# Attention followed by two MLPs on one core: where the 1e-9 of the softmax sum is added, and where the first unit of weights is converted

## The chip, the core and the metric

The kernel runs on one core of a Trainium2 chip. The metric is device time in microseconds (us) of the one launch, and smaller is better. The engines that matter are TensorE (PE, with its weight loads PEld), VectorE (DVE), ScalarE (ACT), GpSimd (POOL) and the sync engine (SP), which issues every DMA of this kernel.

## The reference

Three stages run one after the other, all in float32:

```
q_assign = argmax(q_n . c_n); k_assign = argmax(k_n . c_n)      # 16 clusters per head
scores = 0.125 * q k^T,  -1e9 where the clusters differ         # 2 batches, 8 heads, 768 x 768, head size 64
attn = exp(scores - rowmax);  attn = attn / (sum(attn) + 1e-9)
x = attn @ v                                                    # [1536, 512]
x = max(x@w1, x@w2, x@w3) @ w_out                               # 512 -> 768 -> 512
x = leaky_relu(x@w_in, 0.01) @ w_out                            # 512 -> 2048 -> 512
```

The change touches the `+ 1e-9` of the third line and the preparation of the weights of the fifth.

## The kernel before

**Precision.** Every matmul runs in the float32r format. An operand is split into a high part and a rest (`eh`/`el`, `xh`/`xl`, `wh`/`wl`), and products of the parts are summed in PSUM.

**Attention.** Work comes in 48 units n = 0..47. A unit is 256 queries (two blocks of 128) of one head of one pair of heads; six units make a pair, and there are eight pairs. The letters in `ORDER` name the operations of a unit:

- `S` (L415): four score matmuls of one block of 128 queries; `M` (L422): the row maximum on VectorE; `X` (L428): the exponential on ScalarE, which also writes the row sum.
- `RA` (L438, function `guard`): VectorE adds 1e-9 to the two sums; `RC` (L443): the reciprocal; `RB` (L450): widening on GpSimd.
- `T` (L463): transposes on TensorE; `E`, `B`, `L` (L480, L484, L492, L495): splitting the transposed exponentials into `eh` and `el` on ScalarE, VectorE and GpSimd.
- `V` (L506): twelve matmuls with the values into `o`; `Y`, `K1`, `K2` (L525, L531, L535): out of PSUM into `acc`.
- `G` (L293): similarities to the centroids, two groups of twelve matmuls per pair of heads, for the pair after next.
- `D0`, `D1` (L376): DMAs on SP that stack the operands `q1, q2, k1, k2` of the next pair.

**What sets the order.** The program is written out by hand. `ORDER` has one row of operations for each of the six units of a pair (row r = n mod 6), `op/lag` works on unit n - lag, and `ONCE` adds operations at (unit, position in the row). Every engine runs its own instructions in this order. So an operation that VectorE gets in the middle of a row stands in front of all that VectorE does later in that row.

**Weights.** The MLP weights come in 14 units, each [128, 2048]. A unit is fetched and converted in four pieces c = 0..3 of 512 columns. `Weights.fetch` (L127) issues two DMAs from SP, `raw` and `low`, into one of two slots, taken in turn; a slot is free again once its piece is converted. `Weights.piece` (L144) is a generator of seven VectorE operations (L151, L152, L153, L156, L157, L158, L165; five are TENSOR_SCALAR) and two of ScalarE (L155, L164); each `yield` is a place where it can stop. During attention `take_apart` (L554) advances a piece by one `next` for each `wcX` in `ONCE`. So the pieces of unit 0 are converted in groups of three, three and one operation of VectorE. In the MLP `step` (L167) advances pieces between matmuls.

**MLPs.** From L756 on TensorE runs 36 or 24 matmuls for each chunk of 512 tokens and each weight unit (L782 to L784), with weights of later units converted in between. `split_x` (L771) makes `xh` and `xl` out of `acc` first; its VectorE operations are L774.

Of the kernel before, what the change touches and what calls it, by code (L numbers as in the profile page):

```python
# [8 lines left out]
F32 = mybir.dt.float32  # L9
# [3 lines left out]
ALU = mybir.AluOpType  # L13
AX = mybir.AxisListType
# [3 lines left out]
P = 128  # L18
# [33 lines left out]
ONCE = {  # L52
# [15 lines left out]
}  # L68
WAYS = ("DPP", "DDP", "DPA", "DDP", "DDP", "DPA")
ENGINE = {"QH": "A", "QH@1": "P", "KH": "P", "VH": "P", "KL": "P", "KL@0": "D", "VL": "P", "W": "P", "W@1": "D"}  # L70
WARM = (8, 4, 4, 4)
# [10 lines left out]
def clustered_attention_mlps(  # L82
# [16 lines left out]
    nc = tc.nc  # L99
    PSUM = bass.MemoryType.PSUM  # L100

    const = ctx.enter_context(tc.tile_pool(name="const", bufs=1))
    accp = ctx.enter_context(tc.tile_pool(name="acc", bufs=1))
    wa = ctx.enter_context(tc.tile_pool(name="wa", bufs=1))
# [7 lines left out]
    class Weights:  # L112
# [31 lines left out]
        def piece(self, raw, u, pool, c):  # L144

            high, low = raw[0][:, :, 1], raw[1][:, :, 0]
            x = self.rawp.tile([P, WP], F32, tag="wx", name=f"wx{u}_{c}", bufs=2)
            t = self.rawp.tile([P, WP], F32, tag="wt", name=f"wt{u}_{c}", bufs=3)
            xi, ti, lowf = x.bitcast(U32), t.bitcast(U32), low.bitcast(F32)
            ts, stt = nc.vector.tensor_scalar, nc.vector.scalar_tensor_tensor  # L150
            ts(low, low, 0x01FFFFFF, None, op0=ALU.bitwise_and)  # L151
            ts(xi, high, 0x7FFFFFFF, None, op0=ALU.bitwise_and)  # L152
            ts(x, x, W_LEAST, W_MOST, op0=ALU.max, op1=ALU.min)  # L153
            yield 1.5
            nc.scalar.activation(lowf, low, AF.Copy, scale=2.0**-36)  # L155
            ts(ti, xi, 3, 0x3FFFF000, op0=ALU.logical_shift_left, op1=ALU.bitwise_and)  # L156
            stt(xi, high, 0xC0000000, ti, op0=ALU.bitwise_and, op1=ALU.bitwise_or)  # L157
            ts(ti, xi, 0xFF800000, None, op0=ALU.bitwise_and)  # L158
            yield 2
            if c == 0:  # L160
                wh[u] = pool.tile([P, UW], F32R, tag=f"wh{u % 4}", name=f"wh{u}")
                wl[u] = pool.tile([P, UW], F32R, tag=f"wl{u % 4}", name=f"wl{u}")
            hi, lo = wh[u][:, c * WP : (c + 1) * WP], wl[u][:, c * WP : (c + 1) * WP]
            nc.scalar.copy(hi, x)  # L164
            nc.vector.tensor_tensor(lo, lowf, t, op=ALU.mult)  # L165

        def step(self):  # L167


            passes = 0  # L170
            for _ in range(3):
                self.turn = (self.turn - 1) % 3
                if self.turn == 0:
                    if len(self.going) < 2 and self.todo and self.todo[0][::2] in self.raw:
                        u, pool, c = self.todo.pop(0)
                        g = self.piece(self.raw.pop((u, c)), u, pool, c)
                        self.going.append([0, g])
                at = [g for g in self.going if g[0] == self.turn]
                if at:
                    at[0][0] += 1  # L180
                    passes = next(at[0][1], 0)
                    if not passes:
                        self.going.remove(at[0])
                        passes = 1
                    break
            self.load()
            return passes
# [11 lines left out]
    weights = Weights(wraw, [wraw, wraw])  # L199


    with ExitStack() as att:
# [6 lines left out]
        sm = att.enter_context(tc.tile_pool(name="sm", bufs=2))  # L209
# [7 lines left out]
        gain = const.tile([2 * 2 * C, 1], F32, name="gain")  # L217
        base = const.tile([2 * 2 * C, 1], F32, name="base")
        cb = const.tile([P, NP, 2 * C], F32, name="cb")

        st = {}

# [60 lines left out]
        def bank():  # L283

            st["bank"] = st.get("bank", -1) + 1
            ps = ps_s.tile([P, 1024], F32, tag="s", name=f"s{st['bank']}")
            return ps[:, 0:S], ps[:, S:1024]
# [111 lines left out]
        un = {}  # L399

        def unit(n):
            p, r = divmod(n, 2 * NG)
            j, g = divmod(r, NG)
            return p, j, g

        def scores(n, i):
            p, j, g = unit(n)
            q1, q2, k1, k2 = st[p][j]
            if i == 0:
                un[n] = {"e": [], "sum": sm.tile([P, 2], F32, tag="ssum", name=f"ssum{n}", bufs=4)}  # L410
            c0 = g * G + i * P
            ps, spare = bank()
            for a, b, start in ((q1, k1, True), (q2, k2, False)):
                for lo, hi in ((0, 512), (512, S)):
                    nc.tensor.matmul(  # L415
                        ps[:, lo:hi], a[:, c0 : c0 + P], b[:, lo:hi], start=start, stop=not start
                    )
            un[n]["s", i], un[n]["spare", i] = ps, spare
# [6 lines left out]
        def exps(n, i):  # L425
            u = un[n]
            e = ep.tile([P, S], F32, tag="ee", name=f"ee{n}_{i}")
            nc.scalar.activation(  # L428
                e, u.pop(("s", i)), AF.Exp, bias=u.pop(("m", i)), scale=1.0,
                accum_out=u["sum"][:, i : i + 1],  # L430
            )
            u["e"].append(e)

        def guard(n):
            p, j, g = unit(n)
            if "rs" not in st[p]:
                st[p]["rs"] = sm.tile([P, NG, 2, 2], F32, tag="rs", name=f"rs{p}")
            nc.vector.tensor_scalar_add(st[p]["rs"][:, g, :, j], un[n]["sum"], 1e-9)  # L438

        def inverse(n):  # L440
            p, j, g = unit(n)
# [29 lines left out]
        def way(n, k):  # L471
            return WAYS[n % (2 * NG)][k // 2]

# [79 lines left out]

        def take_apart(op):  # L554

            if op in ("wF", "wL"):
                for c in (0, 1) if op == "wF" else (2, 3):
                    weights.fetch(0, c)
                return
            if op == "wN":  # L560
                for c in (0, 1):
                    weights.fetch(1, c)
                return
            c = int(op[1])
            if c not in pieces:
                pieces[c] = weights.piece(weights.raw[0, c], 0, wa, c)
            next(pieces[c], None)

        def do(op, at):

# [36 lines left out]
            elif o == "D":  # L607
                operands(at, 3 * d)
            elif o == "S":
                scores(at, d)  # L610
            elif o == "M":
                maxima(at, d)
            elif o == "X":
                exps(at, d)
            elif op == "RA":
                guard(at)
# [28 lines left out]
        pieces, scraps = {}, {}  # L645
        with tc.manual_schedule():
# [44 lines left out]

            oh0 = sm.tile([P, D + NQ * 4 * C], BF16, tag="oh", name="oh0", bufs=1)
            nc.vector.memset(oh0[:, 0:D], 0.0)
            st[0]["oh"] = oh0

            def start(op):
# [36 lines left out]
            for n in range(-4 * NG, NU + 6):  # L733
                c, r = divmod(n, 2 * NG)
                items = ORDER[r].split()
                for i in range(len(items) + 1):
# [7 lines left out]
                    if "/" in items[i]:  # L744
                        op, lag = items[i].split("/")
                        at = n - int(lag)
                        if 0 <= at < NU:
                            do(op, at)
                    else:
                        op, ahead = items[i].split("+")  # L750
                        at = c + int(ahead)
# [151 lines left out]
```

## Time and profile before

| | us |
|---|---|
| median of 3 runs | 734.15 (731.75 to 734.33) |
| the profiled execution, its own time | 735.01 |
| its span, first to last instruction | 733.2 |

| engine | busy us | share of the span | instructions |
|---|---|---|---|
| PE | 709.1 | 97% | 3873 |
| PEld | 607.0 | 83% | 3873 |
| DVE | 557.5 | 76% | 1003 |
| ACT | 374.5 | 51% | 717 |
| POOL | 283.8 | 39% | 264 |

The share is an average over two stages: attention up to about 265 us, the MLPs after it. The mean granted clock of TensorE is 0.987 of full speed. In the rows further down, "x4" is a number of instructions, a name on the left of `<-` is written and one on the right is read, and a bracket at a row's end is idle time of that engine just before the instruction with what ended it. Starts are us from the span's start.

### The profile page before, as it was taken

Reading aid. Unit: us, or ns where it says so; the run is one execution under the profiler, and the core shown is the slowest. Engines: PE = TensorE matmul, PEld = TensorE weight load, DVE = VectorE, ACT = ScalarE, POOL = GpSimd, SP = SyncE. Lnnn points to the kernel's source line nnn. Section 1 sums busy time; section 2 is a strip of 40 time slices with the busy share of each in tenths; the row PEclk is TensorE's granted clock in tenths of the full one; section 3 lists DMA queues with packets and bytes.
Section 4 is the critical chain, followed back from the end, with each engine's and each line's share of the span. In section 5 each row is a group of like instructions: output and inputs, shape, how many; then the busy total and the mean of one; then the engine's idle time right before and its main releaser. Section 6 shows DMA issues by size and latency. Waiting matters only on the chain.

```text
span 733.2 us, 10794 instructions
## 1 busy us (share of the span) xinstructions
PE 709.1 (97%) x3873; PEld 607.0 (83%) x3873; DVE 557.5 (76%) x1003; ACT 374.5 (51%) x717; POOL 283.8 (39%) x264
## 2 busy tenths in 40 slices
PE   7999989998999689999999999999999999999997
PEld 5899979987999678888888888888888888888886
DVE  6798999998999988779877289878619954983222
ACT  2788969877899774433323034446434432432220
POOL 1778768776887551011101110323212322222220
PEclk9799999999999999999999999999999999999999
DMA  8976444452444114645556045416414540610112
GB/s 221 284 188 164 99 129 116 111 141 66 107 110 137 58 58 134 232 131 178 161 169 193 8 135 156 149 51 216 162 53 136 179 145 29 199 59 1 44 42 88
DMA packets 30150, 92.37 MB, mean 126 GB/s; under 512 B 4528, under 2 KB 4528, under 8 KB 30096
## 3 DMA queue, kind: packets, MB, share of 16 engines
q1 hardware_dynamic: 30096, 91.67, 42.0%
q8 instruction: 31, 0.51, 0.3%
q14 instruction: 23, 0.19, 0.1%
HBM read 68.16 MB, written 3.15 MB: 97 GB/s over the span
## 4 chain that ended last, share of the span: by engine, by line
PE 86%; DVE 9%; ACT 2%; issue 2%; DMA 0%; POOL 0%; ACTq 0%; POOLq 0%
PE h L784 12%; PE h L783 12%; PE h L782 12%; PE y L783 8%; PE y L782 8%; PE y L784 8%; PE s L415 8%; PE o L506 7%; PE t L463 6%; DVE mx L422 2%; PE s L293 1%; DVE el L492 1%; ACT ee L428 1%; DVE xl L774 1%; DVE rs L438 1%
## 5 line engine op out<-in xcount | busy, mean ns | idle before, releaser
L812 POOL TENSOR_TENSOR hl<-a,hh 128x512 fp32r<-128x512 f32 x66 | 91.0, 1378 | 346.0 <-ACT hh L811 346.0
L784 PE MATMUL h<-xh,wl 128*128 128x512 f32 x408 | 158.9, 389 | 0.0
L782 PE MATMUL h<-xh,wh 128*128 128x512 f32 x408 | 158.8, 389 | 0.0
L783 PE MATMUL h<-xl,wh 128*128 128x512 f32 x408 | 158.7, 389 | 0.0
L811 ACT CAST hh<-a 128x512 fp32r<-128x512 f32 x66 | 41.1, 622 | 127.2 <-DVE a L805 76.4
L782 PE MATMUL y<-hh,wh 128*128 128x512 f32 x264 | 102.7, 389 | 0.0
L783 PE MATMUL y<-hl,wh 128*128 128x512 f32 x264 | 102.7, 389 | 0.0
L784 PE MATMUL y<-hh,wl 128*128 128x512 f32 x264 | 102.7, 389 | 0.0
L428 ACT ACTIVATE ee<-s,mx 128x768 f32<-128x768 f32 x96 | 86.8, 905 | 28.0 <-DVE mx L422 26.8
L495 POOL TENSOR_TENSOR el<-et,eh 128x512 fp32r<-128x512 f32 x72 | 98.2, 1369 | 5.3 <-ACT et L480 2.5
L422 DVE TENSOR_REDUCE mx<-s 128x1 f32<-128x768 f32 x96 | 91.1, 950 | 11.6 <-PE s L415 5.1
L415 PE MATMUL s<-k,q 128*128 128x512 f32 (+3 forms) x384 | 92.9, 366 | 3.5 <-ACT tmp L525 1.8
L783 PEld LDWEIGHTS h<-xl,wh 128*128 128x128 f32 x408 | 76.6, 188 | 15.9
L782 PEld LDWEIGHTS h<-xh,wh 128*128 128x128 f32 x408 | 76.6, 188 | 15.9
L784 PEld LDWEIGHTS h<-xh,wl 128*128 128x128 f32 x408 | 76.6, 188 | 15.8
L803 ACT COPY a<-h 128x512 f32<-128x512 f32 x66 | 38.6, 585 | 94.3 <-PE h L784 92.5
L506 PE MATMUL o<-eh,vs 128*128 128x256 f32 x288 | 75.4, 294 | 11.7 <-DVE acc L535 6.9
L463 PE MATMUL t<-idf,ee 128*128 128x128 f32 x576 | 81.0, 279 | 2.5 <-DVE el L492 2.3
L836 DVE TENSOR_TENSOR acc<-y,acc 128x512 f32<-128x512 f32 x72 | 48.5, 686 | 41.1 <-PE y L784 41.1
L807 DVE SCALAR_TENSOR_TENSOR a<-a,h 128x512 f32<-128x512 f32 x48 | 32.8, 684 | 61.7 <-ACT a L803 61.6
L506 PE MATMUL o<-el,vs 128*128 128x256 f32 x288 | 73.2, 286 | 0.0
L463 PEld LDWEIGHTS t<-idf,ee 128*128 128x128 f32 x576 | 66.7, 145 | 5.8 <-DVE el L492 3.3
(97 smaller groups left out, 1179.2 us busy)
## 6 DMA issues: line engine op xcount, KB each, us to landing
raw<-in_w SPq DMA_DIRECT2D x56, 512.0 KB, 4.2
low<-in_w SPq DMA_DIRECT2D x56, 511.5 KB, 3.5
q<-qh SPq DMA_DIRECT2D x32, 192.0 KB, 3.3
k<-kh SPq DMA_DIRECT2D x32, 192.0 KB, 3.7
rq<-in_qT SPq DMA_DIRECT2D x8, 384.0 KB, 3.7
rk<-in_kT SPq DMA_DIRECT2D x8, 384.0 KB, 3.8
q<-ql SPq DMA_DIRECT2D x16, 192.0 KB, 4.0
k<-kl SPq DMA_DIRECT2D x16, 192.0 KB, 3.5
```

The source lines that it names most:

```text
L415: nc.tensor.matmul(ps[:, lo:hi], a[:, c0 : c0 + P], b[:, lo:hi], start=start, stop=not start)
L422: nc.vector.tensor_reduce(mx, un[n]["s", i], axis=AX.X, op=ALU.max, negate=True)
L428: nc.scalar.activation(e, u.pop(("s", i)), AF.Exp, bias=u.pop(("m", i)), scale=1.0, accum_out=u["sum"][:, i : i + 1],)
L463: nc.tensor.transpose(ps[:, kk, i * P : (i + 1) * P], u["e"][i][:, (k + kk) * P : (k + kk + 1) * P], idf,)
L495: nc.gpsimd.tensor_tensor(lo, et, hi.bitcast(F32), op=ALU.subtract)
L506: nc.tensor.matmul(u["o"], vs[:, t, :], u[e][:, t, :], start=(t == 0 and e == "eh"), stop=(t == NQ - 1 and e == "el"),)
L782: nc.tensor.matmul(ps, ah, bh, start=(k == 0), stop=False)
L783: nc.tensor.matmul(ps, ah, bl, start=False, stop=False)
L784: nc.tensor.matmul(ps, al, bh, start=False, stop=(k == n - 1))
L811: nc.scalar.copy(hh[:, f, :], a)
L812: nc.gpsimd.tensor_tensor(hlo[:, f, :], a, hh[:, f, :].bitcast(F32), op=ALU.subtract)
L836: nc.vector.tensor_tensor(a, ps, a, op=ALU.add)
```

## The change

1. The row sums get four fixed tiles `sums` of [128, 2, 2], filled with 1e-9 once at the start by four memsets on VectorE. The exponential writes its sum into the first of each two numbers, and the 1e-9 stays beside it. `guard` becomes a TENSOR_REDUCE that adds the two, where it was a TENSOR_SCALAR that added a constant.
2. `piece` gets four more `yield`s, so that every VectorE operation of it is a step of its own. `step` runs over the new ones, so the MLP's pace stays.
3. In `ONCE` unit 0's pieces are now `w00`, `w01`, `w02`, `w03`: one step at position 20 of each unit n = 3..9, 10..16, 17..23, 24..30 (before: between n = 14 and n = 51). The fetches stand one by one: `f00`, `f01` at n = 1, `f02` at n = 9, `f03` at 16, and the first two pieces of unit 1 (`f10`, `f11`) at 23 and 30 (before: two at n = 1, two at n = 40, and unit 1's at n = 51).

```diff
-    (0, 7): "KH@1", (0, 8): "QL@1", (1, 11): "wF", (14, 12): "w0a", (15, 20): "w0b",
...
+    (1, 11): "f00", (1, 12): "f01", (3, 20): "w00", (4, 20): "w00", (5, 20): "w00", (6, 20): "w00",
...
             ts(low, low, 0x01FFFFFF, None, op0=ALU.bitwise_and)
+            yield 0
             ts(xi, high, 0x7FFFFFFF, None, op0=ALU.bitwise_and)
+            yield 0
             ts(x, x, W_LEAST, W_MOST, op0=ALU.max, op1=ALU.min)
             yield 1.5
             nc.scalar.activation(lowf, low, AF.Copy, scale=2.0**-36)
             ts(ti, xi, 3, 0x3FFFF000, op0=ALU.logical_shift_left, op1=ALU.bitwise_and)
+            yield 0
             stt(xi, high, 0xC0000000, ti, op0=ALU.bitwise_and, op1=ALU.bitwise_or)
+            yield 0
             ts(ti, xi, 0xFF800000, None, op0=ALU.bitwise_and)
...
-                    passes = next(at[0][1], 0)
+                    passes = next((n for n in at[0][1] if n), 0)
...
+        sums = [const.tile([P, 2, 2], F32, name=f"sums{b}") for b in range(4)]
...
-                un[n] = {"e": [], "sum": sm.tile([P, 2], F32, tag="ssum", name=f"ssum{n}", bufs=4)}
+                un[n] = {"e": [], "sum": sums[n % len(sums)]}
...
-                accum_out=u["sum"][:, i : i + 1],
+                accum_out=u["sum"][:, i, 0:1],
...
-            nc.vector.tensor_scalar_add(st[p]["rs"][:, g, :, j], un[n]["sum"], 1e-9)
+            nc.vector.tensor_reduce(
+                st[p]["rs"][:, g, :, j], un[n]["sum"], axis=AX.X, op=ALU.add
+            )
...
-            if c not in pieces:
-                pieces[c] = weights.piece(weights.raw[0, c], 0, wa, c)
-            next(pieces[c], None)
+            if (u, c) not in pieces:
+                pieces[u, c] = weights.piece(weights.raw.pop((u, c)), u, wa, c)
+            next(pieces[u, c], None)
...
+            for s in sums:
+                nc.vector.memset(s, 1e-9)
```

The order of TensorE's instructions is the same before and after. On VectorE and SP it moves. First, VectorE in unit n = 15 (row 3), before: the guard (L438) and a group of three operations of the first piece (`wt` and `wx` are its working tiles).

```order
L438 TENSOR_SCALAR rs_1354<-ssum_1197 128x2
L422 TENSOR_REDUCE mx_1_1509<-s_1487 128x1
L443 RECIPROCAL rs_1354<-rs_1354 128x2
L438 TENSOR_SCALAR rs_1354<-ssum_1346 128x2
L531 TENSOR_TENSOR acc_64<-o_1473,tmp_1516 64x256
L443 RECIPROCAL rs_1354<-rs_1354 128x2 x2
L156 TENSOR_SCALAR wt_0_1439<-wx_0_1438 128x512
L157 SCALAR_TENSOR_TENSOR wx_0_1438<-raw_0_418,wt_0_1439 128x512
L158 TENSOR_SCALAR wt_0_1439<-wx_0_1438 128x512
L492 TENSOR_TENSOR el_1503<-t_0_1504,eh_1502 128x512
L422 TENSOR_REDUCE mx_0_1572<-s_1519 128x1
```

The same place after, where the guard is L447 and one operation of the second piece (L164) stands.

```order
L447 TENSOR_REDUCE rs_1368<-sums_107 128x2
L431 TENSOR_REDUCE mx_1_1520<-s_1498 128x1
L454 RECIPROCAL rs_1368<-rs_1368 128x2
L447 TENSOR_REDUCE rs_1368<-sums_109 128x2
L542 TENSOR_TENSOR acc_64<-o_1484,tmp_1527 64x256
L454 RECIPROCAL rs_1368<-rs_1368 128x2 x2
L164 TENSOR_SCALAR wt_1_1175<-wx_1_1174 128x512
L503 TENSOR_TENSOR el_1514<-t_0_1515,eh_1513 128x512
L431 TENSOR_REDUCE mx_0_1579<-s_1529 128x1
```

Two of the three operations of the group have gone to other units, and both guards have become reduces.

Second, SP's queue around unit n = 9, before: the operand DMAs of the pair that starts with unit 12. `kl` and `oo` are the operands of its second half of score matmuls, `k_2_0`, `q_2_0` those of its first head.

```order
L376 DMA k_2_1_932<-kh_775 64x768 x2
L376 DMA q_2_1_930<-ql_855 64x768
L376 DMA k_2_0_924<-kl_906 64x768
L376 DMA q_2_0_922<-oo_814 16x768
L376 DMA k_2_0_924<-oo_814 16x768
L376 DMA k_2_1_933<-kl_906 64x768
```

The same place after: `raw_2` and `low_2` are the fetch `f02`, into the slot that the first piece (`low_0`) has held.

```order
L385 DMA k_2_1_938<-kh_780 64x768 x2
L385 DMA q_2_1_936<-ql_861 64x768
L137 DMA raw_2_1097<-in_w 128x2048
L137 DMA low_2_1099<-in_w 128x2046
L385 DMA k_2_0_930<-kl_911 64x768
L385 DMA q_2_0_928<-oo_818 16x768
L385 DMA k_2_0_930<-oo_818 16x768
L385 DMA k_2_1_939<-kl_911 64x768
```

The fetch now stands in front of the six DMAs that finish the pair's operands, and its `low` waits for the last operation of the first piece, at n = 9.

Third, VectorE near the end of attention (units 43 and 44), before: the third and fourth piece among the operations that carry the values out of PSUM (`acc_66<-acc_66,o_3562` is L535).

```order
L531 TENSOR_TENSOR acc_66<-o_3562,tmp_3594 64x256
L443 RECIPROCAL rs_3240<-rs_3240 128x2
L156 TENSOR_SCALAR wt_2_3605<-wx_2_3604 128x512
L157 SCALAR_TENSOR_TENSOR wx_2_3604<-raw_2_3465,wt_2_3605 128x512
L158 TENSOR_SCALAR wt_2_3605<-wx_2_3604 128x512
L535 TENSOR_TENSOR acc_66<-acc_66,o_3562 128x256
L422 TENSOR_REDUCE mx_0_3636<-s_3597 128x1
L492 TENSOR_TENSOR el_3584<-t_0_3585,eh_3583 128x512
L422 TENSOR_REDUCE mx_1_3662<-s_3630 128x1
L151 TENSOR_SCALAR low_3_3471<-low_3_3471 128x512
```

The same place after.

```order
L542 TENSOR_TENSOR acc_66<-o_3556,tmp_3588 64x256
L454 RECIPROCAL rs_3246<-rs_3246 128x2
L546 TENSOR_TENSOR acc_66<-acc_66,o_3556 128x256
L431 TENSOR_REDUCE mx_0_3620<-s_3590 128x1
L503 TENSOR_TENSOR el_3578<-t_0_3579,eh_3577 128x512
L431 TENSOR_REDUCE mx_1_3646<-s_3614 128x1
L542 TENSOR_TENSOR acc_66<-o_3624,tmp_3648 64x256
```

Nothing of the weights stands there any more; the reciprocal is followed at once by the multiplication that frees `o`.

## Rows read from the trace of the kernel before

**Rows 1.** Busy time by stretch: length, then PE, PEld, DVE, ACT, POOL, clock, DMA, GB/s.
```profile
33.40:62.80 29.40, 29.40 (x231) 27.42 (x229) 26.57 (x49) 25.76 (x54) 23.94 (x25) 1.00 0.75 182
92.00:125.50 33.50, 30.18 (x232) 27.59 (x230) 32.02 (x57) 26.37 (x56) 24.82 (x25) 1.00 0.46 115
...
281.00:728.00 447.00, 447.00 (x1974) 370.13 (x1973) 303.47 (x526) 156.22 (x270) 90.98 (x66) 1.00 0.39 124
```
**Rows 2.** The chain that ended last, in order of time: start, length, what.
```profile
33.46 1.26 PE s L293 x12
...
62.85 1.26 PE s L293 x12
...
70.93 0.70 PE s L415 x4
...
73.89 0.89 PE s L415 x4
...
125.55 1.26 PE s L293 x12
...
189.77 1.26 PE s L293 x12
...
257.79 1.29 PE s L415 x4
```
**Rows 3.** Timeline of VectorE: start, length, line, operation, idle before and what ended it.
```profile
5.63 0.09 DVE L693 MEMSET oh<- 128x32 uint32 x1
...
34.76 0.96 DVE L422 TENSOR_REDUCE mx<-s 128x1 f32<-128x768 f32 x1 [1.11 <-PE s L293]
...
57.55 0.43 DVE L531 TENSOR_TENSOR acc<-o,tmp 64x256 f32<-64x256 f32 x1 [0.16 <-ACT tmp L525]
...
100.49 1.67 DVE L156 TENSOR_SCALAR wt<-wx 128x512 uint32<-128x512 uint32 x1
...
265.73 1.05 DVE L438 TENSOR_SCALAR rs<-ssum 128x2 f32<-128x2 f32 x1
```
**Rows 4.** Timeline of GpSimd, 39 us and 100 us.
```profile
39.10 1.81 POOL L250 TENSOR_TENSOR vs<-rv,vs 128x768 fp32r<-128x768 f32 x1
...
100.04 1.83 POOL L250 TENSOR_TENSOR vs<-rv,vs 128x768 fp32r<-128x768 f32 x1
```
**Rows 5.** Timeline of TensorE, the matmuls that it stood idle before, 236 to 272 us.
```profile
240.53 0.36 PE L506 MATMUL o<-eh,vs 128*128 128x256 f32 x1 [2.62 <-DVE acc L535]
...
246.48 0.36 PE L506 MATMUL o<-eh,vs 128*128 128x256 f32 x1 [1.30 <-DVE acc L535]
...
256.57 0.58 PE L506 MATMUL o<-eh,vs 128*128 128x256 f32 x1 [2.25 <-DVE acc L531]
...
267.97 0.36 PE L506 MATMUL o<-eh,vs 128*128 128x256 f32 x1 [1.67 <-DVE acc L535]
```
**Rows 6.** VectorE by line, 33.46 to 62.85 us: busy us, mean ns, idle before.
```profile
L422 DVE TENSOR_REDUCE mx<-s 128x1 f32<-128x768 f32 x12 | 11.4, 952 | 1.8 <-PE s L293 1.5
...
L438 DVE TENSOR_SCALAR rs<-ssum 128x2 f32<-128x2 f32 x6 | 3.8, 632 | 0.1
...
L443 DVE RECIPROCAL rs<-rs 128x2 f32<-128x2 f32 x6 | 0.8, 149 | 0.0
...
L330 DVE TENSOR_REDUCE m_None<-e 128x24 f32<-128x384 f32 x1 | 0.5, 539 | 0.0
```
**Rows 7.** VectorE by line, 18 to 260 us.
```profile
L156 DVE TENSOR_SCALAR wt<-wx 128x512 uint32<-128x512 uint32 x4 | 4.9, 1228 | 0.0
...
L158 DVE TENSOR_SCALAR wt<-wx 128x512 uint32<-128x512 uint32 x4 | 2.6, 649 | 0.1
```
**Rows 8.** Timeline of SP's DMA issues, 61 us.
```profile
61.43 0.46 SPq L376 DMA_DIRECT2D k<-kl  x1
```
**Rows 9.** DMA issues by tile: count, KB each, median us from issue to landing.
```profile
low<-in_w SPq DMA_DIRECT2D x56, 511.5 KB, 3.5
...
k<-oo SPq DMA_DIRECT2D x15, 48.0 KB, 2.8
```

More of the change, by code (lines that the diff above doesn't have):

```diff
@@ L59 @@
     (-3, 27): "N1b@1", (-2, 20): "D2", (-1, 4): "LV1", (-1, 7): "QH@1", (-1, 8): "W@1",
[8 rows of a table removed]
-}
[1 row of a table added]
+}
+ONCE.update({
[6 rows of a table added]
+})
 WAYS = ("DPP", "DDP", "DPA", "DDP", "DDP", "DPA")
@@ L554, in take_apart @@
         def take_apart(op):
-            if op in ("wF", "wL"):
-                for c in (0, 1) if op == "wF" else (2, 3):
-                    weights.fetch(0, c)
+            u, c = int(op[1]), int(op[2])
+            if op[0] == "f":
+                weights.fetch(u, c)
                 return
[L560 to L564, printed above, removed]
-            if c not in pieces:
-                pieces[c] = weights.piece(weights.raw[0, c], 0, wa, c)
-            next(pieces[c], None)
+            if (u, c) not in pieces:
+                pieces[u, c] = weights.piece(weights.raw.pop((u, c)), u, wa, c)
+            next(pieces[u, c], None)
         def do(op, at):
```

13 rows, old and new, of the table ONCE are left out of this document.

## The prediction

> **What bounds the kernel now.** I read the busy time by stretch first [rows 1]. From 281 to 728 us TensorE is busy for all of 447.00 us at full clock: the MLPs are bound by TensorE, and the change leaves its instructions there alone. So the change can gain or lose only in the 281 us before. In an undisturbed pair of heads (33.40 to 62.80) TensorE is also busy all the time, and VectorE for 26.57 of 29.40 us. In a pair that holds a group of weight operations (92.00 to 125.50) VectorE is busy 32.02 us, 5.45 more, and TensorE stands idle for 3.32 of 33.50 us. So VectorE is the second limit in attention, close behind TensorE.
>
> Next the chain of waits, for the pace [rows 2]. The similarity matmuls (L293) mark the same place in each pair: 33.46, 62.85, 125.55, 189.77. The first two are 29.39 us apart, with no weight operations between them. The next marks span two pairs each: 62.70 and 64.22 us against 2 x 29.39 = 58.78. So the first piece of the weights cost 3.92 us and the second 5.44, together 9.36.
>
> The timeline of VectorE in the undisturbed pair [rows 3] shows how much idle time there is: four waits, from 1.11 us at 34.76 to 0.16 at 57.55, 2.15 us in all. This gives a simple account that can be checked: 5.45 us more work, of which 2.15 fit into the idle time, leave 3.3 us, and 3.92 were lost. I price the change with it: what VectorE gets beyond its idle time, TensorE loses.
>
> Why a weight operation is dear here: the one at 100.49 takes 1.67 us [rows 3]. GpSimd has an operation from 100.04 to 101.87 [rows 4], and the VectorE operation ends 0.29 us after that. It has waited for GpSimd.
>
> The third and fourth piece stand at the end of attention, and TensorE's own idle rows show their price [rows 5]: 2.62, 1.30 and 2.25 us in front of value matmuls, behind VectorE's L535 and L531, 6.17 in all. After the last the clock drops: four score matmuls at 257.79 take 1.29 us against 0.70 at 70.93 [rows 2], the lower of the two levels (1.2 against 2.4 GHz). From 256.57 to 259.9 this costs 3.3 x (1 - 0.70 / 1.29) = 1.5 us. So these two pieces cost 7.67 us, and the four pieces together 17.0.
>
> **The change part by part.**
>
> The guard. Six in the undisturbed pair take 3.8 us, 632 ns each [rows 6]. A reciprocal of the same 128x2 takes 149 ns, so most of the guard is waiting. The new TENSOR_REDUCE over 2 x 2 inputs isn't in the trace. Two reduces bound it: 952 ns for 768 inputs and 539 for 384, 1.08 ns for an input, so 539 - 380 x 1.08 = 130 ns from below and 539 from above. I take 150, the value of the reciprocal, which is nearest in size. GpSimd is busy 23.94 of 29.40 us [rows 1] and the reduces show no wait, the row maxima with a mean of 952 over twelve. Relief for each pair: 6 x (632 - 150) = 2.89 us.
>
> The Trainium skill (VectorE: DVE Perf Modes, section Rules for kernel authors) calls tensor_reduce the slowest VectorE operation and advises against it where time matters. By that the guard would cost 539 ns as a reduce does here, and the relief would shrink to 0.56 us for each pair. Another of its pages (SBUF — State Buffer, section Who interferes with whom) says that on this chip tensor_reduce never contends with GpSimd while tensor_scalar can. The trace agrees with the second so far (952 ns on average beside a busy GpSimd), and I follow the rows' slope.
>
> The weight operations, one to a unit. The seven kinds, four of each, from L156 with 4.9 us to L158 with 2.6, sum to 26.0 us for 28, 0.93 us each [rows 7]. From below, 0.65 (L158's mean); from above, 1.67 for every one. I take 0.93, since a single one meets GpSimd as the grouped ones do: in row 3 of the order it falls on GpSimd's 39.10 to 40.91 [rows 4] and must wait like the one at 100.49, elsewhere less. Six in a pair: 5.57 us. Against them stand 2.15 of idle time and 2.89 of relief, so 0.53 us for each pair are left over. Units 3 to 30 are 28/6 = 4.67 pairs: 2.5 us lost. Against 9.36 before.
>
> The fetch at n = 9. On SP `low_2` now stands ahead of six operand DMAs and waits for the last operation of the first piece. Before, the first of the six was issued at 61.43 [rows 8], and the score matmuls that need them start at 73.89, the third of four near 74.3 [rows 2]. Now: GpSimd's operation of row 3 falls one pair later, at 39.10 + 29.39 = 68.49, and ends at 70.3; the weight multiplication ends near 71.0; the fetch and the first head's three DMAs need 4 x 0.46 us of issue, so the last starts at 72.4 and lands 2.8 us later [rows 9], at 75.2. TensorE waits 0.9 us, or up to 4.4 if the fetch's 3.5 us lie fully in front. From below, nothing, if VectorE runs ahead. I take 1.5. The fetches at 16, 23 and 30 stand before loads or operands needed three or more units (some 15 us) later, which hides them. Unit 1's early fetch meets an MLP start that is bound by TensorE: nothing.
>
> The end of attention. The 7.67 us of the two pieces go. The guard at 265.73 takes 1.05 us [rows 3] in front of the L535 for which TensorE waits 1.67 at 267.97 [rows 5]: 0.9 back. Late next is the chain through GpSimd and VectorE's `split_x`, of which two operations now stand earlier in the order, 0.7 us each, in place of a weight operation: I take 1.0 off, between 0 and 2. So 7.6 us gained.
>
> Four memsets at the start: one takes 0.09 us [rows 3], at most 0.4 in all, in front of an operation that waits for GpSimd: nothing.
>
> The sum: 9.36 - 2.5 - 1.5 + 7.6 = 13.0 us gained. The profiled execution took 735.01 us, so 722.0; the median is 0.86 lower, so 721.1.
>
> **The rivals.**
>
> *All is hidden.* If a single operation costs under 0.84 us, the 5.04 us of room hold six of them; with no stall at the fetch and nothing late at the end the gain is 9.36 + 7.67 + 0.9 = 17.9: 716 us. For it: GpSimd idles 5.46 of 29.40 us in a pair [rows 1], and an operation that meets it idle waits for nothing. Against it: the account has understated the loss once (3.3 against 3.92).
>
> *VectorE stays over its limit.* At 1.1 us an operation, 1.56 us are left in each pair, 7.3 in all; the fetch stalls 4.0 and the end gives 6.6. Gain 9.36 - 7.3 - 4.0 + 6.6 = 4.7: 729.4 us. For it: the operations stand alone among GpSimd's, where a group's later ones may have found it idle.
>
> *The guard gets no cheaper*, because the reduce waits too or is slow in itself. Without the 2.89, 3.42 us are left in each pair, 16.0 in all: 9.36 - 16.0 - 1.5 + 6.7 = 1.4 us lost, 735.6 us. Against it: the reduces' means [rows 6].
>
> *Slower: every single operation runs into a GpSimd operation.* At the 1.67 us of the row at 100.49, six cost 10.0 us in a pair, 5.0 over the room, 23.3 in all; against the 15.4 us that the rest gains that is 7.9 us lost, 742 us. It decides from 1.39 us an operation, where 4.67 x (6 x 1.39 - 5.04) = 15.4. For it: in row 3 it is certain. Against it: that is one operation of six, and the grouped ones averaged 0.93 beside the same GpSimd. The page on the SBUF named above has the rule behind it: whoever takes the shared port second waits until the other's instruction is done.
>
> **How the numbers follow.** The forecast has 0.56, all hidden 0.15, VectorE over its limit 0.17, no cheaper guard 0.07, slower 0.05. The forecast's own range, with 0.8 to 1.05 us an operation and 0 to 3 us at the fetch, is 717 to 726. The range of 716 to 730 reaches to the second and third case and leaves out the last two. A measurement of this kernel can tell 0.5%, 3.7 us, from no change; the first three cases are beyond that except the slow edge of the third. Faster 0.86, same 0.09, slower 0.05.
>
> **What would show it.** Right: the guard at 0.15 us without spread; TensorE idle less than 1 us in each pair between 33 and 190 us; 62.85's mark moved by under 1 us and 189.77's to about 184; no idle time behind L535 and L531 before 258; the first MLP matmul near 252 instead of 265. A stall of score matmuls near 74 us behind a DMA would show the fetch. Wrong: a mean weight operation above 1.2 us; a guard that keeps its spread; TensorE's idle time moved into units 3 to 30 rather than gone.

## The result and the profile after

The changed kernel takes 727.50 us (median of five runs, 724.77 to 728.75), against 734.15 us before (731.75 to 734.41). The ratio is 0.9916, with a 95% interval of 0.9888 to 0.9943: it is faster by 6.65 us. The forecast was 721.1 us with a range of 716 to 730. The direction was right and the time lies in the range, but the gain is only about half of the 13.0 us of the sum. The forecast's own range, 717 to 726, misses the time; only the wide range, stretched to two of the rivals, holds it.

The profiled execution of after took 724.77 us, 10.24 less than that of before. I divide both by three marks in TensorE's timeline: the similarity matmuls of the units n = 2 and n = 32, and the first MLP matmul.

| stretch | before, us | after, us | gain | forecast |
|---|---|---|---|---|
| start to n = 2 | 33.30 | 31.21 | 2.1 | 0 |
| n = 2 to n = 32, five pairs | 156.31 | 157.28 | -1.0 | 5.4 |
| n = 32 to the first MLP matmul | 75.29 | 67.52 | 7.8 | 7.6 |
| MLPs | 468.3 | 467.0 | 1.3 | 0 |

The first and last rows belong to the executions as much as to the kernels. From 20 to 30 us TensorE's granted clock is 0.61 in before's profile and 1.00 in after's; in two other kernels with the new guard, below, it is 0.66, and n = 2 comes at 34.5 and 34.9 us. This profiled execution is also the shortest of after's five. The two middle rows give 6.8 us, and the medians differ by 6.65.

So the end came as forecast, and the pairs did not. The chain of waits of after, with the marks that answer to [rows 2]:

```profile
31.38 1.26 PE s L302 x12
...
62.90 1.26 PE s L302 x12
95.00 1.26 PE s L302 x12
...
126.29 1.26 PE s L302 x12
...
157.59 1.26 PE s L302 x12
...
188.66 1.26 PE s L302 x12
```

Every pair now takes 31.1 to 32.1 us, where an undisturbed one took 29.39 and the forecast was 29.9. The windows of the first and the third of these pairs of after (columns as in [rows 1]):

```profile
31.38:62.90 31.52, 29.72 (x231) 27.43 (x230) 28.49 (x53) 26.18 (x54) 23.83 (x26) 1.00 0.70 169
95.00:126.29 31.29, 29.53 (x232) 27.43 (x230) 29.43 (x56) 26.56 (x55) 24.90 (x26) 1.00 0.60 156
```

TensorE stands idle for 1.8 us in each, and VectorE, with 29.43 of 31.29 us busy, still has 1.86 us of idle time. By the forecast's account that time should have been used up before TensorE lost any. VectorE by line, 18 to 200 us (columns as in [rows 6, 7]):

```profile
L431 DVE TENSOR_REDUCE mx<-s 128x1 f32<-128x768 f32 x71 | 67.4, 951 | 12.2 <-PE s L302 8.9 <-PE s L360 1.2 <-PE s L424 0.9
...
L447 DVE TENSOR_REDUCE rs<-sums 128x2 f32<-128x4 f32 x35 | 5.1, 145 | 0.3
...
L171 DVE TENSOR_TENSOR wl<-low,wt 128x512 fp32r<-128x512 f32 x4 | 4.1, 1031 | 0.0
L157 DVE TENSOR_SCALAR wx<-wx 128x512 f32<-128x512 f32 x4 | 3.8, 942 | 0.0
...
L160 DVE TENSOR_SCALAR wt<-wx 128x512 uint32<-128x512 uint32 x4 | 2.8, 710 | 0.0
```

The two prices are close to the forecast: the guard (L447) takes 145 ns, and the weight operations, whose dearest and cheapest kinds stand here, average 0.87 us over all 28. The first row tells where VectorE's idle time is: of 12.2 us in front of the row maxima, 8.9 end with the similarity matmuls, L302. These stand in two of the six units of a pair.

Where the pair loses its time shows in the chain of waits of after, 106 to 126 us, that is from the unit n = 16 (row 4) to the next mark:

```profile
106.04 0.71 PE s L424 x4
106.75 0.02 issue
106.77 0.96 DVE mx L431
107.73 0.60 DVE wl L171
...
112.81 1.31 DVE low L153
...
116.70 0.95 DVE mx L431
117.65 0.70 DVE wx L155
...
118.95 1.37 DVE ql L256
...
122.74 0.33 issue
123.07 1.16 DVE wx L157
...
124.97 0.63 PE t L474 x4
```

From the pair's start to 106.75 every piece of the chain is TensorE's. After it, for 18 us, VectorE runs from operation to operation and TensorE follows, through rows 4, 5, 0 and 1. Three of the four weight operations in it stand in rows 5, 0 and 1 (112.81, 117.65, 123.07) and make 3.17 us of the chain; the pair is 2.3 us longer than one without any (28.97 us in e3, below). TensorE's idle rows show the same stretch (timeline, 94 to 128 us):

```profile
115.73 0.35 PE L360 MATMUL s<-idb,oh 128*64 128x128 bf16 x3 [1.11 <-DVE oh L353]
...
122.26 0.97 PE L424 MATMUL s<-k,q 128*128 128x512 f32 x4 [0.35 <-ACT ee L437]
...
124.97 0.63 PE L474 MATMUL t<-idf,ee 128*128 128x128 f32 x4 [0.30 <-DVE rs L447]
```

And VectorE's in that pair (95 to 126 us) are these three, the last of them at 106.01:

```profile
96.30 0.96 DVE L431 TENSOR_REDUCE mx<-s 128x1 f32<-128x768 f32 x1 [0.86 <-PE s L302]
...
102.17 0.96 DVE L431 TENSOR_REDUCE mx<-s 128x1 f32<-128x768 f32 x1 [0.34 <-PE s L302]
...
106.01 0.69 DVE L503 TENSOR_TENSOR el<-t,eh 128x512 fp32r<-128x512 f32 x1 [0.19 <-ACT eh L491]
```

### The profile page after: what moved, and what is told of

Same layout as the page of the kernel before. It is cut to its first block, busy times and chain, and to the rows that moved or that the text cites. A ratio compares the mean times of both kernels' runs of the same rounds, so it can differ in the third digit from the quotient of the medians.

```text
span 723.0 us, 10801 instructions
## 1 busy us (share of the span) xinstructions
PE 701.3 (97%) x3872; PEld 601.0 (83%) x3873; DVE 541.8 (75%) x1007; ACT 373.9 (52%) x717; POOL 281.2 (39%) x264
## 4 chain that ended last, share of the span: by engine, by line
PE 81%; DVE 14%; ACT 2%; issue 1%; DMA 1%; SPq 1%; POOL 0%; DVEq 0%; ACTq 0%
PE h L792 13%; PE h L790 13%; PE h L791 13%; PE y L792 8%; PE y L791 8%; PE y L790 8%; PE t L474 5%; PE s L424 5%; PE o L517 5%; DVE mx L431 4%; PE s L302 2%; DVE el L503 2%; DVE ql L256 1%; DVE acc L542 1%; ACT ee L437 1%
## 5 line engine op out<-in xcount | busy, mean ns | idle before, releaser
L506 POOL TENSOR_TENSOR el<-et,eh 128x512 fp32r<-128x512 f32 x72 | 94.5, 1320 | 3.5 <-ACT et L491 0.8
L437 ACT ACTIVATE ee<-s,mx 128x768 f32<-128x768 f32 x96 | 86.9, 905 | 17.3 <-DVE mx L431 16.7
L424 PE MATMUL s<-k,q 128*128 128x512 f32 (+3 forms) x384 | 89.1, 354 | 5.2 <-ACT ee L437 3.9
L474 PE MATMUL t<-idf,ee 128*128 128x128 f32 x576 | 78.4, 275 | 1.7 <-DVE rs L447 1.7
L517 PE MATMUL o<-eh,vs 128*128 128x256 f32 x288 | 73.4, 288 | 3.2 <-DVE acc L546 1.8
L517 PE MATMUL o<-el,vs 128*128 128x256 f32 x288 | 71.7, 282 | 0.0
L474 PEld LDWEIGHTS t<-idf,ee 128*128 128x128 f32 x576 | 65.2, 142 | 4.3 <-PE o L517 2.4
```

What stands on the lines that cost most here:

```text
L424: nc.tensor.matmul(ps[:, lo:hi], a[:, c0 : c0 + P], b[:, lo:hi], start=start, stop=not start)
L437: nc.scalar.activation(e, u.pop(("s", i)), AF.Exp, bias=u.pop(("m", i)), scale=1.0, accum_out=u["sum"][:, i, 0:1],)
L474: nc.tensor.transpose(ps[:, kk, i * P : (i + 1) * P], u["e"][i][:, (k + kk) * P : (k + kk + 1) * P], idf,)
L506: nc.gpsimd.tensor_tensor(lo, et, hi.bitcast(F32), op=ALU.subtract)
L517: nc.tensor.matmul(u["o"], vs[:, t, :], u[e][:, t, :], start=(t == 0 and e == "eh"), stop=(t == NQ - 1 and e == "el"),)
```

## The experiments

Two theories were set against each other. **Room**: a pair has so much idle time of VectorE, and work fits into it wherever it stands (the forecast's account); then the operations must cost more than they seem to. **Place**: the idle time lies in rows 2 and 3, behind the similarity matmuls, and an operation of rows 4, 5, 0 or 1 costs its length. The marks of all kernels, in us, from TensorE's timelines (the stretches of the table above), are these. The ratios are to runs of before on the same chip: their median is 733.70 us for e1, e2, e3 and e5 (19 runs) and 733.95 for e4 and e7 (12 runs).

| kernel | median | ratio to before, interval | start to n = 2 | n = 2 to 32 | n = 32 to MLP |
|---|---|---|---|---|---|
| before | 734.15 | 1 | 33.30 | 156.31 | 75.29 |
| after | 727.50 | 0.9916 (0.9888 to 0.9943) | 31.21 | 157.28 | 67.52 |
| e1_guard_only | 726.12 | 0.9884 (0.9856 to 0.9911) | 34.93 | 147.91 | 73.68 |
| e2_spread_only | 733.90 | 1.0006 (0.9993 to 1.0019) | 33.32 | 163.86 | 68.89 |
| e3_no_weights | 719.72 | 0.9808 (0.9789 to 0.9826) | 38.65 | 144.83 | 67.52 |
| e5_rows501 | 733.41 | 0.9995 (0.9981 to 1.0008) | 31.31 | 165.13 | 67.53 |
| e4_rows23 | 717.24 | 0.9768 (0.9733 to 0.9803) | 32.15 | 149.26 | 68.52 |
| e7_three_rows501 | 729.47 | 0.9929 (0.9904 to 0.9955) | 34.54 | 156.56 | 69.35 |

**The guard alone** (e1): before with the first part of the change, the weights as they were.

```diff
+        sums = [const.tile([P, 2, 2], F32, name=f"sums{b}") for b in range(4)]
...
-            nc.vector.tensor_scalar_add(st[p]["rs"][:, g, :, j], un[n]["sum"], 1e-9)
+            nc.vector.tensor_reduce(
+                st[p]["rs"][:, g, :, j], un[n]["sum"], axis=AX.X, op=ALU.add
+            )
...
+            for s in sums:
+                nc.vector.memset(s, 1e-9)
```

> The kernel before with the guard as a reduce beside a fixed 1e-9; the weights' groups stay where they were. Two theories of why single operations of 0.87 us, less than the 0.93 forecast, still cost about 2 us in each pair. Room (the account of the prediction): a pair's idle time of VectorE and what the guard gives back hold any work, wherever it stands; then the two pairs with a group lose 5.45 - 5.04 = 0.4 us each instead of 3.9 and 5.4, and the time is near 724 us. Place: VectorE's idle time lies in rows 2 and 3 alone, behind the similarity matmuls, and from row 4 to row 1 it runs without a gap; then only the guards next to the groups help, 1 to 1.5 us in each of the two pairs and 1 to 2 at the end, and the time is 729 to 731.

Measured: 726.12 us, which lies between the two; the guard by itself gives 7.6 us, and by the intervals of the table it can't be told from the whole change. A pair that meets the first piece only in its last 1.9 us, and the next, which holds the rest of it (windows of e1 between marks):

```profile
63.90:92.86 28.96, 28.96 (x230) 27.35 (x229) 25.02 (x50) 25.60 (x54) 23.83 (x25) 1.00 0.50 131
...
92.86:123.37 30.51, 29.43 (x230) 27.37 (x229) 29.15 (x55) 26.22 (x56) 24.58 (x25) 1.00 0.48 123
```

The second row has 4.13 us more of VectorE's work and is only 1.55 us longer. The groups of three stand at n = 14 and 15 (for the second piece at 26 and 27), which are rows 2 and 3. So the old places of the first two pieces, where the change took the operations away, were the cheap ones. The first row surprises too: like e1's pair before it, which has no weight operation (34.93 to 63.90), it is 0.43 us shorter than an undisturbed pair of before, in which TensorE was busy without a gap [rows 1]. The chain of before shows where that was hidden: in row 4 four score matmuls take 0.88 us, and in row 5 twelve value matmuls 1.63, where the same two take 0.69 and 1.43 in e1.

```profile
44.50 0.88 PE s L415 x4
...
50.46 1.63 PE o L506 x12
```

Waits as short as these, inside a group of matmuls, count as busy time in these views. With the old guard VectorE already held up TensorE in an undisturbed pair, and [rows 1] could not show it; the 0.89 us at 73.89 in [rows 2] could have.

**The spread alone** (e2): after, with the old guard back.

```diff
-            nc.vector.tensor_reduce(
-                st[p]["rs"][:, g, :, j], un[n]["sum"], axis=AX.X, op=ALU.add
-            )
+            nc.vector.tensor_scalar_add(st[p]["rs"][:, g, :, j], un[n]["sum"], 1e-9)
```

> The changed kernel with the old guard (a TENSOR_SCALAR). Room: each pair has 6 x 0.87 - 2.15 = 3.1 us too much, 14.3 over 4.67 pairs against 9.4 before, and the end gives 7.7: near 731 us. Place: the operations and the guards of rows 4 to 1 both stand in a stretch without a gap, so each pair loses about 2.1 for the operations there and 1.7 to 2.2 for the guards' waits, 18 to 20 in all: 735 to 738 us.

Measured: 733.90 us, again between the two, and no change from before. The spread takes 6.4 us from the end of attention (75.29 to 68.89) and adds 7.6 to the pairs (156.31 to 163.86). All of the gain of after is the guard's: 733.90 - 727.50 = 6.4 us. Here the old guard averages 370 ns, not 582 as before from 18 to 200 us: the weight operations take 1.01 us each, where they take 0.87 in after. That part of the guards' waiting went over to them is a reading of these means and not shown.

**No weights in attention** (e3): after, with unit 0's conversion left out in `take_apart` and its weights set to zero, so the MLPs compute with zeros there.

```diff
+            if u == 0:
+                return
```

> The changed kernel without the conversion of the first unit of weights (seven operations of VectorE and two of ScalarE for each piece; its weights are zeros). Both theories: pairs of 29.4 us, TensorE without idle time, 10 us less than the changed kernel: 717 to 718. Its use is the map: place expects gaps of VectorE of 1 us behind the similarity matmuls of rows 2 and 3 and, from row 4 to row 1, only small ones that the guards have left, under 3 us in a pair. If the pairs stay above 30 us, something else than the weight operations slows them, the fixed tiles of the sums for instance.

Measured: 719.72 us, 2 us above the expectation. The mark n = 2 comes at 38.65 us, which I lay to the zero fill on GpSimd (two memsets, 3.6 us from 3.67 us on); that isn't shown. All five pairs take 28.97 us. That is the base: the 28 operations cost after 157.28 - 144.83 = 12.45 us, of their 24.3 us of busy time. The window of one pair of e3:

```profile
67.60:96.57 28.97, 28.97 (x230) 27.36 (x229) 24.52 (x49) 25.61 (x55) 23.83 (x25) 1.00 0.65 167
```

VectorE's idle rows in the same pair:

```profile
69.08 0.96 DVE L431 TENSOR_REDUCE mx<-s 128x1 f32<-128x768 f32 x1 [1.58 <-PE s L302]
71.09 0.36 DVE L313 TENSOR_REDUCE m<-s 128x12 f32<-128x192 f32 x1 [0.46 <-ACT ee L437]
74.94 0.96 DVE L431 TENSOR_REDUCE mx<-s 128x1 f32<-128x768 f32 x1 [1.00 <-PE s L302]
78.79 0.69 DVE L503 TENSOR_TENSOR el<-t,eh 128x512 fp32r<-128x512 f32 x1 [0.19 <-ACT eh L491]
96.04 0.42 DVE L542 TENSOR_TENSOR acc<-o,tmp 64x256 f32<-64x256 f32 x1 [0.42 <-ACT tmp L536]
```

The forecast's room of 5.04 us was too large: these waits add up to 3.65 us, counted as the forecast counted its 2.15 (all time in which VectorE isn't busy, with gaps too short to be listed, is 4.45). And 3.04 us of it lie in the 7 us behind the two groups of similarity matmuls (the first three rows); from 79 to 95.6 us no row shows any.

**Six operations in rows 5, 0 and 1** (e5): two in each of these units and none in rows 2 to 4. The edit against after, for the first pair:

```diff
-    (3, 20): "w00", (4, 20): "w00", (5, 20): "w00", (6, 20): "w00", (7, 20): "w00", (8, 20): "w00",
+    (5, 18): "w00", (5, 20): "w00", (6, 20): "w00", (6, 22): "w00", (7, 18): "w00", (7, 20): "w00",
```

> The changed kernel with the same 28 operations over the same units, but two in each unit of rows 5, 0 and 1 and none in rows 2, 3 and 4. Room: a pair holds the same six operations, so 31.3 us and 727 as the changed kernel. Place: three more operations of 0.87 us stand in the stretch without a gap, 33 to 34 us for a pair, 8 to 12 us more: 735 to 739.

Measured: 733.41 us, 5.9 above after, with the same operations and nearly as many to a pair (four in the last). It is less than place expected, and far from room. The first three pairs, at full clock, take 32.3 to 33.1 us, 3.3 to 4.1 over the base for six operations. The last two take 33.8, and not for their operations alone: TensorE's granted clock is 0.86 from 150 to 162 us and 0.89 from 180 to 196.

**Three operations in rows 2 and 3** (e4): two in row 2, one in row 3, in front of the waits (the first pair holds one alone); what is left over is done at n = 32, 33 and 38 to 47, in all rows in the end. Some of the entries, against after:

```diff
+    (3, 24): "w00", (8, 17): "w00 w00", (9, 24): "w00", (14, 17): "w00 w00", (15, 24): "w00", (16, 2): "f02",
...
+    (32, 17): "w01 w02", (33, 24): "w02", (34, 2): "f03", (38, 17): "w02 w02", (39, 20): "w02",
```

> The changed kernel with the same 28 operations in the two rows where VectorE waits: three in a pair, two ahead of the row maximum behind the similarity matmuls of row 2 and one at the same place of row 3, and the last twelve over units 38 to 47, where there are no similarities. Place: pairs stay at 29.0 us, as without any weights, and the time is 714 to 717, faster than both kernels (the run without weights started some 5 us late because of its fill of zeros). Room: the same, three operations of 0.87 us against 4.45 us of idle time in a pair. If pairs go over 29.5 us, both are wrong.

Measured: 717.24 us (713.91 to 721.08, six runs): faster than before by 16.7 us and than after by 10.3, and 0.2 above the expected range. The marks, in the chain of waits of e4:

```profile
65.33 1.26 PE s L321 x12
...
94.32 1.26 PE s L321 x12
...
181.57 1.26 PE s L321 x12
```

The first of these pairs takes 28.99 us and the three after it 87.25, 29.08 each: the base to within 0.1, with three operations in each. One pair's operations, in VectorE's timeline:

```profile
93.96 0.67 DVE L181 SCALAR_TENSOR_TENSOR wx<-raw,wt 128x512 uint32<-128x512 uint32 x1
94.66 0.94 DVE L183 TENSOR_SCALAR wt<-wx 128x512 uint32<-128x512 uint32 x1
95.62 0.96 DVE L450 TENSOR_REDUCE mx<-s 128x1 f32<-128x768 f32 x1
...
100.41 1.93 DVE L190 TENSOR_TENSOR wl<-low,wt 128x512 fp32r<-128x512 f32 x1
102.26 0.94 DVE L450 TENSOR_REDUCE mx<-s 128x1 f32<-128x768 f32 x1
```

They are hardly cheaper in themselves than in the next run, 1.05 us on average over these four pairs against 1.20 there; the third even takes 1.93 us. They fill the time in which the row maximum behind them would have waited (the brackets of 1.58 and 1.00 us in e3 are gone). Only the first pair, 32.15 to 65.16, is long: score matmuls at 45.94 wait 2.23 us for a DMA, and the granted clock is 0.66 from 45 to 50 us. SP is already 3 us later than in after at its first weight fetch (23.25 against 20.23 us), long before the first weight operation at 38.40. Why is open.

**The same three in rows 5, 0 and 1** (e7): as e4, one operation in each of these rows. Some of the entries, against e4:

```diff
-    (3, 24): "w00", (8, 17): "w00 w00", (9, 24): "w00",
+    (5, 20): "w00", (6, 20): "w00", (7, 20): "w00", (11, 20): "w00",
```

> As the kernel with three operations in a pair in rows 2 and 3, but the three stand one each in rows 5, 0 and 1; units 38 to 47 are the same. Room: no difference between the two, 2.6 us of work against 4.45 us of idle time: 714 to 717. Place: rows 4 to 1 hold at most 1 us, so 1.6 us more for each of five pairs, 8 us: 722 to 725.

Measured: 729.47 us, 12.2 more than e4 and 4.5 above the upper end that place gave. Room expected the two to be alike; place expected a difference of some 8 us. In the profiles the five pairs make 7.3 us of it although e4's first pair is long (e7 has 15 operations in them, e4 13), the start 2.4 and the end 0.8; the start has a granted clock of 0.66 from 20 to 30 us, against 0.89 in e4, so the pairs alone are to be compared. The third pair of e7, in its chain of waits:

```profile
97.25 1.26 PE s L324 x12
...
111.76 0.43 DVE acc L564
...
114.75 1.58 DVE wl L193
...
119.86 0.71 DVE low L175
...
125.28 1.16 DVE wx L177
...
128.51 1.26 PE s L324 x12
```

VectorE still has listed waits of 2.50 us in this pair, all before 108.3 us, and TensorE loses 2.3 us all the same. A pair takes 31.3 us on average, 2.3 over the base, for three operations. That is also the length of after's pairs, where three more stand in rows 2 to 4. So of the six operations of after, those in rows 2 to 4 are nearly free and those in rows 5, 0 and 1 cost about 0.8 us each, of the 1.2 us that one takes there in e7. The rows were not tried one by one. Place holds, with one correction: row 4 is nearly free as well. Its operation at 107.73 in after is in the chain of waits, but in e7, without it, VectorE's part of the chain only begins later, in row 5, and the pair is no shorter.

## Why the prediction was wrong where it was

- **The guard**: right. 145 ns against the 150 taken, without the old spread. The Trainium skill (VectorE: DVE Perf Modes, section Rules for kernel authors) calls tensor_reduce the slowest VectorE operation. For this size the traces say otherwise: the reduce takes 145 ns, the TENSOR_SCALAR at least 148 and 582 on average, most of it waiting; and e1 shows 7.6 us of gain. Following the rows was right.
- **The weight operations**: right in size, 0.87 us against 0.93. The rival with 1.1 us an operation came out at 729.4, close to the measured 727.5, but for another reason: its price was not there. That the range holds the time is luck in this sense.
- **The step that failed**: "what VectorE gets beyond its idle time, TensorE loses", with idle time and relief added up over the pair (2.15 + 2.89 us of room for 5.57 of work, 0.53 lost). The room was too large by 1.4 us, 3.65 in e3: of the 2.89 us that the guards were to give back, 1.50 came as waits and 0.43 as a shorter pair. But no size of the room explains the runs. The three operations of e7 take 3.6 us in a pair, would fit into it and cost 2.3; the three of e4 take 3.1 and cost 0.1. It is the place that decides: VectorE works in the program's order, and the idle time of rows 2 and 3 is past when the operations of rows 5, 0 and 1 come. The loss is 2.1 to 3.1 us a pair, where 0.53 was taken. Over the five pairs that is 12.45 us against 2.5 and the fetch's 1.5: 8.4 too few. The base was 28.97 instead of 29.40 (2.2 us over five pairs in the change's favour), which leaves the 6.3 us by which the stretch missed (-1.0 against 5.4).
- **Why the check of the account misled**: it was tried on before's first piece, 3.3 us worked out and 3.92 found. Six of its seven operations stand at n = 14 and 15, just where the idle time is, so the check could not tell room from place. The rows to see it were there: the longest wait in [rows 3] ends with L293, and [rows 6] gives 1.5 of 1.8 us to it.
- **The second piece's 5.44 us before**: 1.5 of them are TensorE's clock. From 154.79 to 189.61 TensorE stands idle for 3.32 us, as in the first piece's pair; but its granted clock is 0.66 from 170 to 175 us, where the first piece's pair has 1.00 throughout.
- **The fetch at n = 9**: the stall is there, behind the DMA that was named, and smaller: 0.59 us against 1.5. In TensorE's timeline of after:

```profile
74.88 0.59 PE L424 MATMUL s<-k,q 80*128 80x512 f32 x2 [0.59 <-DMA k<-oo]
```

- **The end**: right as a sum, 7.8 us against 7.6. The guard alone gives 1.6 of it (e1) where 0.9 was taken, and moving the pieces away the rest. But TensorE still waits behind VectorE three times (L542 and L546 are the old L531 and L535), and the sign that was named, no such wait before 258 us, failed. TensorE's timeline of after:

```profile
253.03 0.39 PE L517 MATMUL o<-eh,vs 128*128 128x256 f32 x1 [1.39 <-DVE acc L542]
...
257.87 0.35 PE L517 MATMUL o<-eh,vs 128*128 128x256 f32 x1 [0.46 <-DVE acc L546]
...
263.83 0.36 PE L517 MATMUL o<-eh,vs 128*128 128x256 f32 x1 [1.32 <-DVE acc L546]
```

- **The signs that were named**: TensorE idle under 1 us in a pair was wrong (1.8), and so were 189.77's mark at 184 (188.66) and the first MLP matmul near 252 (256.01). One sign of being wrong came true: TensorE's idle time went into the units 3 to 30. Together they point at the pairs. 62.85's mark moved by only 0.05 us, as was said, but by chance: the pair is 2.1 us longer and began 2.1 us earlier. A mark has to be read from the mark before it.

What stays open: the DMA that is late in e4's first pair, and the last three waits above. Without the first, e4's profiled execution, 719.25 us, would gain some 4 us more (33.01 us against 29.00); whether its other executions, 713.91 to 721.08 us, have that wait is not shown.

## What to carry to other kernels

Idle time of an in-order engine is a place, not an amount: before work is moved into it, list the engine's waits with their times, and put the work right in front of them. Then read the chain of waits for stretches that the second engine runs through without a gap; there an added operation can cost most of its length (2.3 us for 3.6 of work here), however much idle time the loop shows as a whole. A bottleneck that is "busy all the time" may still be waiting within its groups: compare the same group's length at several places.

## What the runs showed of the hardware

- Beside a busy GpSimd a TENSOR_SCALAR of only 128x2 elements took 148 to 1259 ns (before), and a TENSOR_REDUCE of 128x4 took 128 to 158 ns (48 in after). The Trainium skill (SBUF — State Buffer, section Who interferes with whom) says of tensor_reduce on this chip that it never contends with GpSimd; the trace agrees.
- The same operation of two inputs in SBUF, `wl<-low,wt`, took from 0.67 us (181.21 in e4) to 1.93 us (100.41 in e4).
- The clock granted from 20 to 30 us differs between executions: 0.61, 0.66, 0.66 and 1.00 in the profiles of before, e1, e7 and after. The mark n = 2 comes 2.1 to 3.7 us later in the first three than in after (in e2, with 1.00 there but 0.68 from 10 to 20 us, also 2.1 us later), so parts of two profiles should be compared from a mark behind the start.
